# One pair of rotation tables, and a fixed engine for each step of the rotation, in an attention and two-MoE kernel

## The chip, the cores and the metric

The kernel runs on one NeuronCore of a Trainium2 chip. Its engines are TensorE (PE in the profile; PEld is its weight load), VectorE (DVE), ScalarE (ACT), GpSimd (POOL) and SyncE (SP), which here issues the DMA transfers. The metric is the device time of one execution in microseconds, lower is better.

## The reference

Attention over batch 4, 8 heads, 576 positions, head size 64, with rotary embedding of queries and keys; then a dense MoE layer with squared ReLU, then a second MoE layer with 8 experts of which each token takes one.

```python
def rotate(x):
    x1, x2 = (x[..., :half], x[..., half:])
    return np.concatenate([x1 * cos - x2 * sin, x1 * sin + x2 * cos], axis=-1)
q_rot, k_rot = (rotate(q), rotate(k))
scores = scale * np.matmul(q_rot, k_rot.transpose(0, 1, 3, 2))
scores = scores - np.max(scores, axis=-1, keepdims=True)
attn = np.exp(scores)
attn = attn / (np.sum(attn, axis=-1, keepdims=True) + 1e-09)
attn_out = np.matmul(attn, v)
...
h = x @ w_in;  r = np.maximum(h, 0.0);  x = (r * r) @ w_out     # 2304 x 512, d_ff 2048
...
for e in range(E):                                              # 8 experts, F 1024
    h = np.maximum(x[mask] @ w1[e], 0.0)
    out[mask] = gate_w[mask, None] * eom[mask, e, None] * (h @ w2[e])
```

## The kernel before

**Precision.** TensorE multiplies in fp32r. Each fp32 operand is split into a high part (a cast to fp32r) and a low part (the operand less its high part), and products are added up from two or three of the combinations. So nearly every tile in front of TensorE costs one cast and one subtraction.

**Attention.** The 32 heads are worked in 16 pairs p. `prepare(p)` loads the pair's keys and queries (`load(i)`: i = 1 for the keys, 0 for the queries), swaps neighbouring rows (`swap`, VectorE), multiplies x and the swapped x by a table each (`mul`, L295), adds them (`add`, L299) and splits the result. The table tile `tabs` has four parts of 128 x 576: cosine and sine times −1/√64 for the queries, cosine and sine for the keys. Each is a transfer of its own, in the first pair only. For the keys the high and low part go into the tile `hl` (`high_k`, `low_k`), and `fan(j)` copies them by DMA (L324, four transfers for a pair) into the operand tile `d`, to both halves of the partitions. For the queries `high_q` and `low_q` write `d` directly, one half of the partitions (one head) at a time. `ends_` copies the last 64 query rows of both heads into the tile `dz`. The values are split into `vh` (`v_high`, `v_low`).

`unit(P, p, c)` then does for each of five query chunks: `scores` (PE, L401, L409), the row minimum (`least`, DVE, L416; scores carry the minus sign), the exponential (`exponential`, ACT, L422), transposes of the probabilities (`turned`, L456; `remainder`, L461), their high part `phi` (cast, L209) and low part `plo` (DVE, L212), and the product with the values (L557 to L562). Line 209 is the helper for all casts and copies of ACT and DVE, L207 the one for POOL, L212 the one for all subtractions; in the profile they are told apart by the tiles.

**Which engine.** The strings `ROPE`, `SPLIT`, `TURN` and `SHIFT` name for every pair and step an engine (v VectorE, a ScalarE, p GpSimd). Before, they are long and differ from pair to pair; the first pair has strings of its own.

**The order.** Nothing is ordered by hand. `plan.add(engine, cost, emit, key, deps, slots)` notes each step; `Plan.emit` goes through a model of the engines in which each one takes, of the steps that are ready, the one with the lowest key, and writes the instructions in the order of the planned starts. On the chip every engine, and SyncE's queue of transfers, runs its instructions in that order, each waiting for its data. `KEYS` holds the keys by kind of step, `TAIL` and `LATE` those of the last block's rows and of the late units. Costs are in ns.

**The MoE stages.** Weights of the first MoE come as raw 64-bit words and are converted by ACT and DVE (`add_conversion`: L662 to L693, and L212 into `pg`), two half steps for each of 16 slices f. Two slices have pages from the start, two more once all pairs are prepared (`gate0`), twelve once the attention is over (`gate1`). `add_block(0)` starts when the first tokens' sums are loaded back and split (POOL, L754, L757, L212 into `xlo`); L787 and L817 are its products. Blocks 1 to 4, the routing and the expert units follow.

Of the kernel before, what the change touches and what calls it, by code (L numbers as in the profile page):

```python
# [40 lines left out]
BIG_MAX = (NT - EARLY * (BLK[3][0] // E) + E * 127) // UNIT  # L41
NH = 2 * (EARLY + LATE_MAX)
KF = F2 // 128
ROPE, SPLIT, TURN, SHIFT = "ppvpvvvpppvppppvvppppvpppppvppppppppppppppvpppppvpppppppppppppppppppppppvppppppppppppppppppppppp", "pppvvvaappvppappapppppppavppapvvppppavpppppappapppppapaappapppppapppppappappppaappppappppppappvp", "vvaavaaaavaaavaaaaaaavaaaaaaaaavavaaavaaaaaaaaaaavaaaaaaavaavaaaaaaavvvaaaaaaaavvvaaaaavaaaaaaavaaaaaaaaavvaavaaaaaaaaaaaaavaaaavaaaaaaaaavaaaaaaaavaaaaavaaaaaaaaavavaaaaaaaaaaavaaaaaaaavaaaaa", "aaaaaaaaaaaaaaaaaaaavaaaaavaavvaaaaaaaaaaaavaavaaaaaaavaaaaaaaav"
F64_TINY = 1.125 * 2.0**-15


TAIL, LATE = -10142, -11286
HI, LO = "aaavaaav", "vpvvvpvv"
DMA_RATE = 241  # L50
AHEAD = dict(DVE=10, ACT=14)
BEGIN = (4, 6, 6, 1)
SECOND = "ap"
KEYS = dict(fan=-84975, swap=32320, step=73908, conv=54493, x0=22475, end=-86588, load=-5688, rope=106951, qk=-63351, v=-40073, s=-11980, min=4893, exp=18765, rc=-77484, t=9315, hi=9602, lo=-12270, pv=18619, x=-74523)


def f32(ap):
    return ap.bitcast(F32)
# [18 lines left out]
def act(n):  # L77
    return 93 + n / 1.2
# [119 lines left out]
def two_moe_kernel(ctx, tc, qk, v, tab, cst, w_in, w_out, wg, w1, w2, out):  # L198
# [51 lines left out]
    def add_attention(ctx, rest, first):  # L250
# [21 lines left out]
        def prepare(p):  # L272
# [8 lines left out]
            def load(i):  # L281

                if "x" not in T:
                    T["x"] = pre.tile([128, 4, S], F32, tag="x", name="x", bufs=2)
                sp.dma_start(out=T["x"][:, 2 * i], in_=qk[p, :, i])
                if first:
                    for z in (2 * i, 2 * i + 1):
                        sp.dma_start(out=tabs[:, z], in_=tab[:, z])

            def swap(i):  # L290
                ve.stream_shuffle(out=T["x"][:, 2 * i + 1], in_=T["x"][:, 2 * i], mask=[j ^ 1 for j in range(32)])  # L291
# [1 line left out]
            def mul(i):  # L293
                x = T["x"]
                eng(3 * (i // 2) + i % 2).tensor_tensor(out=x[:, i], in0=x[:, i], in1=tabs[:, i], op=ALU.mult)  # L295
# [5 lines left out]
            def operand():  # L301
                if "d" not in T:
                    T["d"] = two.tile([128, 2, 3, S], F32R, tag="d", name="d")
                return T["d"]
# [12 lines left out]
            def low_q(j, on):  # L317
                h, o = slice(64 * j, 64 * j + 64), slice(64 - 64 * j, 128 - 64 * j)
                sub(ve if on == "v" else po, T["d"][o, j, 0], T["x"][h, 0], f32(T["d"][h, j, 0]))

            def fan(j):
                h = slice(64 * j, 64 * j + 64)
                for u in (0, 64):
                    sp.dma_start(out=f32(operand()[u:u + 64, j, 1:3]), in_=f32(T["hl"][h]))  # L324

            on, split = ("vvvvvv", "aavvap") if first else (choice(ROPE, p, 6), choice(SPLIT, p, 6))
            eng = lambda i: ve if on[i] == "v" else po
# [2 lines left out]
            parts = {}  # L330
            for i in (1, 0):
                k = key + KEYS["rope"] - i
                o = plan.add("SP", 3670 if first else 1220, lambda i=i: load(i), key + KEYS["load"] - i, fanned, [xs])
                m = [plan.add("DVE", dve(S), lambda i=i: swap(i), key + KEYS["swap"] - i, [o], [xs])]
                m.append(plan.add(*price(3 * i), lambda z=2 * i: mul(z), k, [o, m[0]], [xs]))
                m[0] = plan.add(*price(3 * i + 1), lambda z=2 * i + 1: mul(z), k, m[:1], [xs])
                o = plan.add(*price(3 * i + 2), lambda i=i: add(i), k, m, [xs])
                k = key + KEYS["qk"] - i
                if i:
                    a = plan.add(*copy_price(split[1], S), high_k, k, [o], [xs, hls])  # L340
                    b = plan.add(*sub_price(split[3], S), low_k, k, [a], [xs, hls])
                    T["fan"] = [plan.add("SP", 2444, lambda j=j: fan(j), key + KEYS["fan"], [a, b], [hls, ds]) for j in range(2)]
                    if first:
                        fanned.append(~T["fan"][1])
                else:
                    T["q"] = []
                    for j in range(2):
                        e = split[0] + split[2] if j == 0 else SECOND[2 * (p % (len(SECOND) // 2)):][:2]
                        if first:
                            e = "av" if j else "av"  # L350
                        a = plan.add(*copy_price(e[0], S), lambda j=j, e=e: high_q(j, e[0]), k, [o], [xs, ds])
                        b = plan.add(*sub_price(e[1], S), lambda j=j, e=e: low_q(j, e[1]), k, [a], [xs, ds])
                        T["q"].append([a, b])
# [16 lines left out]
            zs = ring_z.take()  # L370

            def ends_():
                copy(
                    on_ends, out=ends_q.rearrange("p j (a q) -> p (j a) q", a=2)[:, 0:4:3], in_=f32(T["d"][:, :, 0, 512:S])
                )

            on_ends = "a" if p == 0 else "p"
            T["end"] = plan.add(*copy_price(on_ends, 128), ends_, key + KEYS["end"], T["q"][0] + T["q"][1] + zeros, [ds, zs])
            T["slots"] = ds, vs, ring_sm.take(), zs
            prepared.extend([*T["fan"], *T["q"][0], *T["q"][1], T["vl"]])  # L380
            begin.append(T["fan"])
            return T

        def unit(P, p, c):
# [7 lines left out]
            for j in range(1 if both else 2):  # L392
                ss = ring_s.take()

                def scores(j=j):
                    d = P["d"]
                    t = T["s", j] = ps_s.tile([128, 2, 512], F32, tag="s", name="sc")
                    for hf in range(2):
                        z = slice(hf * HB, hf * HB + HB)
                        for part in (1, 2):  # L400
                            te.matmul(  # L401
                                out=t[:, hf, 0:HB], lhsT=ends_q[:, 1] if both else d[:, j, 0, q0:q0 + n],
                                rhs=d[:, 1 if both else j, part, z], start=part == 1, stop=part == 2 and not both,
                            )
                        if both:

                            for o, k0, m in ((0, 512, 64), (64, 0, HB - 64)) if hf == 0 else ((0, HB - 64, HB),):
                                for part in (1, 2):
                                    te.matmul(  # L409
                                        out=t[:, hf, o:o + m], lhsT=ends_q[:, 0], rhs=d[:, 0, part, k0:k0 + m],  # L410
                                        start=False, stop=part == 2 and o + m == HB,
                                    )

                def least(j=j):
                    T["mx", j] = small.tile([128, 1], F32, tag="mx", name="mx")
                    ve.tensor_reduce(out=T["mx", j], in_=T["s", j][:, :, 0:HB], axis=AX.XY, op=ALU.min)  # L416

                def exponential(j=j):
                    if j == 0:
                        T["pt"] = two.tile([128, 2, S], F32, tag="p", name="pt", bufs=3)  # L420
                    i = 5 * j + c
                    se.activation(  # L422
                        out=T["pt"][:, j].rearrange("p (a b) -> p a b", a=2), in_=T["s", j][:, :, 0:HB],
                        func=AF.Exp, bias=T["mx", j], scale=-1.0, accum_out=sums[p % 2][:, i:i + 1],
                    )

                ds, _, sms, zs = P["slots"]
                if both:
                    a = plan.add("PE", 1270, scores, key + KEYS["s"], [P["end"], *P["fan"]], [ss, ds, zs])
                else:  # L430
                    a = plan.add("PE", 4 * pe(HB), scores, key + KEYS["s"], [P["fan"][j], *P["q"][j]], [ss, ds])
                b = plan.add("DVE", 667, least, key + KEYS["min"], [a], [ss])
                ends.append(plan.add("ACT", 730, exponential, key + KEYS["exp"], [b] + ends, [ss, ps_, sms]))
                scored.append(ends[-1])
                P.setdefault("ends", []).append(ends[-1])
# [1054 lines left out]
def _shape_constants():  # L1490
# [3 lines left out]
    cos, sin = np.cos(freqs).T, np.sin(freqs).T  # L1494
    c = np.tile(np.stack([cos, cos], axis=1).reshape(D, S), (2, 1))
    s = np.tile(np.stack([-sin, sin], axis=1).reshape(D, S), (2, 1))
    g = np.float32(-1.0 / np.sqrt(D))
    tab = np.stack([c * g, s * g, c, s], axis=1).astype(np.float32)
    tab[64:, 2:] = np.roll(tab[64:, 2:], 64, axis=2)
    cst = np.zeros((128, 128 + 256 + E + 128 + NH + NRT), np.float32)  # L1500
    cst[:, 0:128] = np.eye(128)
    cst[:, 128:256] = np.triu(np.ones((128, 128)), 1)
# [12 lines left out]
def _layout(q, k, v, moe_w_in, moe_w_out, moe2_w_gate, moe2_w_output_gate, moe2_w1, moe2_w2):  # L1515

    qk = np.stack([q, k]).reshape(2, NP, 2, S, 2, D // 2).transpose(1, 2, 5, 4, 0, 3).reshape(NP, 128, 2, S)
    qk[:, 64:, 1] = np.roll(qk[:, 64:, 1], 64, axis=2)
    vp = v.reshape(NP, 2, S, D)
    vl = np.zeros((NP, 128, 11, D), v.dtype)  # L1520
    for j in range(2):
# [29 lines left out]
```

## Time and profile before

| | |
|---|---|
| median of 3 runs | 1007.44 us (1007.02 to 1008.35) |
| the profiled execution | 1005.06 us |
| its span, first to last instruction | 1003.2 us |
| busy: TensorE, VectorE, ScalarE, GpSimd | 933.9, 717.0, 529.7, 355.3 us |
| TensorE's mean granted clock | 0.992 of full speed |
| DMA | 117.70 MB, mean 117 GB/s |

Busy time is the time in which an engine executes; the rest of the span it waits or has nothing to do. Instructions of one engine may overlap a little at their ends, so that the sum of their durations is above its busy time. "x <- y" in a row means that the instruction writes x and reads y, or, in brackets behind an idle time, that y released the engine.

### The profile page before, as it was taken

The numbers are of one execution on the slowest core, as the hardware profiler recorded it, in microseconds if no ns is written. First come the engines' busy times: TensorE is split into PE (matmuls) and PEld (weight loads), VectorE is DVE, ScalarE is ACT, GpSimd is POOL, SyncE is SP. The second block draws the span as 40 slices with busy tenths as digits, with TensorE's granted clock in tenths as the row PEclk, the third lists the DMA queues.
The fourth block names the chain that finished last, engine by engine and source line by source line (L and its number), as shares of the span: only waits on it lengthen the run. The fifth ranks groups of instructions, "written<-read, shape, count | busy, mean of one in ns | idle before, by whom it ended". The sixth has DMA issues, their size and how long they took to land.

```text
span 1003.2 us, 16374 instructions
## 1 busy us (share of the span) xinstructions
PE 933.9 (93%) x5612; PEld 818.5 (82%) x5612; DVE 717.0 (71%) x1346; ACT 529.7 (53%) x1109; POOL 355.3 (35%) x277
## 2 busy tenths in 40 slices
PE   0799889998999999999999999999999999999995
PEld 0689888898888888778877887788998898999985
DVE  4989999999999999753255225444586999366666
ACT  1688878897888778521232123212463455244443
POOL 1789966998956000000000000000031455134342
PEclk9999999999999999999999999999999999999998
DMA  6466755765656665130022003000560613452611
GB/s 178 115 164 191 182 162 145 188 165 153 179 138 185 215 222 176 51 118 1 0 86 72 1 1 90 6 0 22 181 219 23 219 54 100 144 166 89 206 53 34
DMA packets 56616, 117.70 MB, mean 117 GB/s; under 512 B 9137, under 2 KB 18881, under 8 KB 56513
## 3 DMA queue, kind: packets, MB, share of 16 engines
q1 hardware_dynamic: 53232, 105.94, 36.1%
q0 software_dynamic: 3280, 10.49, 3.2%
q8 instruction: 52, 0.85, 0.4%
q14 instruction: 52, 0.42, 0.1%
HBM read 99.55 MB, written 19.21 MB: 118 GB/s over the span
## 4 chain that ended last, share of the span: by engine, by line
PE 71%; DVE 10%; ACT 5%; DMA 5%; issue 3%; POOL 3%; SPq 2%; DVEq 0%; POOLq 0%; ACTq 0%
PE h L787 20%; PE a L817 19%; PE h L1305 10%; PE a L1342 10%; PE sc L401 4%; DVE plo L212 2%; PE tp L456 2%; ACT pt L422 2%; DVE mx L416 2%; PE ov L557 2%; ACT phi L209 1%; POOL x L295 1%; DVE pg L212 1%; PE m L894 1%; DMA d<-hl 1%
## 5 line engine op out<-in xcount | busy, mean ns | idle before, releaser
L787 PE MATMUL h<-xhi,pg 128*128 128x512 f32 (+1 forms) x640 | 198.8, 374 | 0.0
L817 PE MATMUL a<-gh,pg 128*128 128x512 f32 (+1 forms) x640 | 196.2, 373 | 0.0
L1259 POOL DMA_INDIRECT raw<-x1d,gidx x22 | 22.7, 1033 | 373.8 <-DVE ssc L243 356.8
L794 ACT ACTIVATE r<-h 128x512 f32<-128x512 f32 (+1 forms) x80 | 44.3, 554 | 192.0 <-PE h L787 178.6
L401 PE MATMUL sc<-d 128*128 128x288 f32 x512 | 100.8, 321 | 41.2 <-DVE d L212 24.4
L787 PEld LDWEIGHTS h<-xhi,pg 128*128 128x128 f32 x640 | 117.3, 188 | 23.1
L817 PEld LDWEIGHTS a<-gh,pg 128*128 128x128 f32 x640 | 117.2, 188 | 22.1
L802 DVE TENSOR_TENSOR r<-r 128x512 f32<-128x512 f32 (+1 forms) x64 | 40.1, 626 | 124.1 <-ACT gh L798 124.1
L817 PE MATMUL a<-gl,pg 128*128 128x512 f32 (+1 forms) x320 | 119.6, 374 | 1.9 <-DVE gl L212 1.7
L422 ACT ACTIVATE pt<-sc,mx 128x576 f32<-128x576 f32 x144 | 107.5, 748 | 23.8 <-DVE mx L416 22.8
L1305 PE MATMUL h<-raw,pg 128*128 128x256 f32 x960 | 117.8, 283 | 2.1 <-ACT y L1349 1.3
L1305 PEld LDWEIGHTS h<-raw,pg 128*128 128x128 f32 x960 | 116.6, 191 | 3.4 <-issue 1.7
L787 PE MATMUL h<-xlo,pg 128*128 128x512 f32 (+1 forms) x320 | 118.9, 372 | 0.0
L401 PEld LDWEIGHTS sc<-d 128*128 128x128 f32 x512 | 75.5, 195 | 50.5 <-DVE d L212 24.8
L416 DVE TENSOR_REDUCE mx<-sc 128x1 f32<-128x576 f32 x144 | 105.8, 748 | 5.0 <-PE sc L401 4.5
L212 DVE TENSOR_TENSOR plo<-tp,phi 128x512 fp32r<-128x512 f32 x144 | 95.9, 678 | 4.4 <-ACT phi L209 3.7
L212 DVE TENSOR_TENSOR pg<-pg,pg 128x512 fp32r<-128x512 f32 x102 | 92.7, 933 | 4.1 <-ACT pg L209 3.7
L456 PE MATMUL tp<-ident,pt 128*128 128x128 f32 x576 | 87.5, 279 | 3.4 <-DVE plo L212 3.0
L295 POOL TENSOR_TENSOR x<-x,tabs 128x576 f32<-128x576 f32 x51 | 77.8, 1538 | 9.5 <-DVE x L291 4.7
L209 ACT CAST phi<-tp 128x512 fp32r<-128x512 f32 x125 | 72.2, 588 | 14.4 <-PE tp L456 13.8
L212 POOL TENSOR_TENSOR pg<-pg,pg 128x512 fp32r<-128x512 f32 x34 | 47.6, 1403 | 87.4 <-ACT pg L209 87.3
L456 PEld LDWEIGHTS tp<-ident,pt 128*128 128x128 f32 x576 | 70.1, 143 | 6.0 <-issue 2.4
(224 smaller groups left out, 1761.7 us busy)
## 6 DMA issues: line engine op xcount, KB each, us to landing
pg<-w_dram SPq DMA_DIRECT2D x176, 256.0 KB
d<-hl SPq DMA_DIRECT2D x64, 288.0 KB
x<-qk_dram SPq DMA_DIRECT2D x32, 288.0 KB
xtd<-xt SPq DMA_DIRECT2D x32, 288.0 KB
raw<-w_in_dram SPq DMA_DIRECT2D x16, 512.0 KB
raw<-w_out_dram SPq DMA_DIRECT2D x16, 512.0 KB
vr<-v_dram SPq DMA_DIRECT2D x16, 352.0 KB
x1d<-b SPq DMA_DIRECT2D x18, 256.0 KB
```

Source lines behind the costliest of these rows:

```text
L209: (ve.tensor_copy if on == "v" else se.copy)(out=out, in_=in_)
L212: eng.tensor_tensor(out=out, in0=a, in1=b, op=ALU.subtract)
L295: eng(3 * (i // 2) + i % 2).tensor_tensor(out=x[:, i], in0=x[:, i], in1=tabs[:, i], op=ALU.mult)
L401: te.matmul(out=t[:, hf, 0:HB], lhsT=ends_q[:, 1] if both else d[:, j, 0, q0:q0 + n], rhs=d[:, 1 if both else j, part, z], start=part == 1 ...
L416: ve.tensor_reduce(out=T["mx", j], in_=T["s", j][:, :, 0:HB], axis=AX.XY, op=ALU.min)
L422: se.activation(out=T["pt"][:, j].rearrange("p (a b) -> p a b", a=2), in_=T["s", j][:, :, 0:HB], func=AF.Exp, bias=T["mx", j], scale=-1.0, ...
L456: te.transpose(out=t[:, k], in_=T["pt"][:, j, i:i + 128], identity=ident)
L787: te.matmul(out=G["t"], lhsT=a[:, 128 * c:128 * c + 128], rhs=m[:, c, :n], start=c == 0 and i == 0, stop=c == KC - 1 and i == 2,)
L794: se.activation(out=G["r"], in_=G["t"], func=AF.Relu)
L817: te.matmul(out=T["acc", d][:, :n], lhsT=a[:, 128 * d:128 * d + 128], rhs=m, start=f == 0 and i == 0, stop=f == NF - 1 and i == 2,)
L1305: te.matmul(out=T["t"][:, f], lhsT=m[:, z], rhs=r[:, c], start=i == 0, stop=i == 11)
L1342: te.matmul(out=T["t"], lhsT=a[:, k, 128 * i:128 * i + 128], rhs=m, start=k == 0 and y == 0, stop=k == KF - 1 and y == 2,)
```

## The change

The tables come as one pair, cosine and sine, in one transfer; the queries' pair is made of it on ScalarE (`scale_tables`). To use one pair for both, the queries of the second head are now laid out with the same roll by 64 positions as its keys. In the first pair the keys' parts are no longer copied by DMA: `first_high` (ScalarE) and `first_low` (VectorE) write them to both halves of the partitions, and the load of the queries hangs in the plan on the keys' sum. From the second pair on GpSimd does all products and sums of the rotation, all subtractions for keys, queries and values and the high part of the values, and ScalarE all other high parts, all casts of the probabilities and all copies of the output. `ends_` is two copies instead of one. All keys have new values.

```diff
-ROPE, SPLIT, TURN, SHIFT = "ppvpvvvpppvppppvvppppvpppppv...", "pppvvvaappvppappap...", "vvaavaaaavaaavaa...", "aaaaaaaaaaaaaaaaaaaavaaaaavaavv..."
+ROPE, SPLIT, TURN, SHIFT = "pppppp", "aapppp", "aaaaaaaaaaaa", "aaaa"
-TAIL, LATE = -10142, -11286
+TAIL, LATE = -332229, -479512
-KEYS = dict(fan=-84975, swap=32320, step=73908, conv=54493, x0=22475, end=-86588, load=-5688, rope=106951, qk=-63351, v=-40073, s=-11980, min=4893, exp=18765, rc=-77484, t=9315, hi=9602, lo=-12270, pv=18619, x=-74523)
+KEYS = dict(fan=-213982, swap=238988, step=201344, conv=238593, x0=399905, end=-631240, load=-373541, rope=-65135, qk=-119699, v=-65126, s=-122507, min=-216773, exp=-122385, rc=-253869, t=350365, hi=-152247, lo=-190621, pv=489233, x=-165917)
...
                 sp.dma_start(out=T["x"][:, 2 * i], in_=qk[p, :, i])
-                if first:
-                    for z in (2 * i, 2 * i + 1):
-                        sp.dma_start(out=tabs[:, z], in_=tab[:, z])
+                if first and i:
+                    sp.dma_start(out=tabs[:, 2:4], in_=tab)
...
+            def first_high(j, u):
+                h, o = slice(64 * j, 64 * j + 64), slice(64 * u, 64 * u + 64)
+                se.copy(out=operand()[o, j, 1], in_=T["x"][h, 2])
+
+            def first_low(j, u):
+                h, o = slice(64 * j, 64 * j + 64), slice(64 * u, 64 * u + 64)
+                sub(ve, operand()[o, j, 2], T["x"][h, 2], f32(T["d"][h, j, 1]))
...
+            def scale_tables():
+                se.activation(out=tabs[:, 0:2], in_=tabs[:, 2:4], func=AF.Copy, scale=-(D ** -0.5))
...
-                o = plan.add("SP", 3670 if first else 1220, lambda i=i: load(i), key + KEYS["load"] - i, fanned, [xs])
+                o = plan.add("SP", 3670 if first and i else 1220, lambda i=i: load(i), key + KEYS["load"] - i, fanned, [xs])
+                if first and i:
+                    tables = plan.add("ACT", act(2 * S), scale_tables, key + KEYS["qk"], [o], [])
+                ready = [tables] if first and not i else []
...
-                if i:
+                if i and first:
+                    T["fan"] = []
+                    for j in range(2):
+                        made_ = []
+                        for u in range(2):
+                            a = plan.add("ACT", act(S), lambda j=j, u=u: first_high(j, u), k, [o], [xs, ds])
+                            made_ += [a, plan.add("DVE", dves(S), lambda j=j, u=u: first_low(j, u), k, [a], [xs, ds])]
+                        T["fan"].append(made_)
+                    fanned.append(o)
+                elif i:
...
-                    if first:
-                        fanned.append(~T["fan"][1])
...
-    g = np.float32(-1.0 / np.sqrt(D))
-    tab = np.stack([c * g, s * g, c, s], axis=1).astype(np.float32)
-    tab[64:, 2:] = np.roll(tab[64:, 2:], 64, axis=2)
+    tab = np.stack([c, s], axis=1).astype(np.float32)
+    tab[64:] = np.roll(tab[64:], 64, axis=2)
...
-    qk[:, 64:, 1] = np.roll(qk[:, 64:, 1], 64, axis=2)
+    qk[:, 64:] = np.roll(qk[:, 64:], 64, axis=3)
```

## Rows read from the trace of the kernel before

**Rows 1.** The page: busy us (share of the span) and instructions of TensorE first.

```profile
PE 933.9 (93%) x5612; PEld 818.5 (82%) x5612; DVE 717.0 (71%) x1346; ACT 529.7 (53%) x1109; POOL 355.3 (35%) x277
```

**Rows 2.** Stages from:to: length, busy us of each engine, clock, DMA share, GB/s.

```profile
40.00:320.00 280.00, 258.05 (x1923) 242.14 (x1922) 267.45 (x452) 236.03 (x566) 229.26 (x175) 0.99 0.64 170
326.00:417.00 91.00, 90.91 (x398) 73.83 (x397) 88.54 (x159) 68.85 (x121) 0.00 (x0) 1.00 0.53 169
```

**Rows 3.** Chain that ended last, first 30 us: start, length, what.

```profile
1.64 3.62 DMA tabs<-tab_dram
...
5.28 0.77 DVE x L295
...
6.07 0.77 DVE x L299
...
8.35 0.54 SPq L324
...
11.93 1.33 SPq L285
...
29.12 0.62 DVE mx L416
```

**Rows 4.** The opening in order of time: start, length, engine, line, operation.

```profile
0.72 0.40 SPq L285 DMA_DIRECT2D x<-qk_dram  x1
...
3.58 0.79 DVE L291 STREAM_SHUFFLE x<-x 128x576 f32<-128x576 f32 x1
...
7.57 0.76 DVE L212 TENSOR_TENSOR hl<-x,hl 128x576 fp32r<-128x576 f32 x1 [0.74 <-ACT hl L209]
...
19.78 0.76 DVE L295 TENSOR_TENSOR x<-x,tabs 128x576 f32<-128x576 f32 x1 [0.96 <-DMA tabs<-tab_dram]
...
21.36 1.36 ACT L209 CAST d<-x 64x576 fp32r<-64x576 f32 x2
...
22.98 2.71 DVE L212 TENSOR_TENSOR d<-x,d 64x576 fp32r<-64x576 f32 x2
...
23.87 1.33 PE L401 MATMUL sc<-d 128*128 128x288 f32 x4 [23.87 <-DVE d L212]
```

**Rows 5.** GpSimd's groups, 0 to 330 us: busy us, mean ns, idle before.

```profile
L295 POOL TENSOR_TENSOR x<-x,tabs 128x576 f32<-128x576 f32 x51 | 77.8, 1538 | 9.5 <-DVE x L291 4.7 <-issue 3.7 <-POOL d L212 0.7
L299 POOL TENSOR_TENSOR x<-x 128x576 f32<-128x576 f32 x30 | 45.9, 1532 | 19.4 <-DVE x L295 18.9
L212 POOL TENSOR_TENSOR d<-x,d 64x576 fp32r<-64x576 f32 x30 | 42.9, 1428 | 3.1 <-ACT d L209 0.8
...
L207 POOL TENSOR_SCALAR dz<-d 128x128 fp32r<-128x128 f32 x15 | 6.0, 400 | 3.1 <-PE sc L409 3.0
L207 POOL TENSOR_SCALAR d<-x 64x576 fp32r<-64x576 f32 x8 | 5.8, 730 | 0.3
...
L207 POOL TENSOR_SCALAR vh<-vr 128x704 fp32r<-128x704 f32 x6 | 5.1, 845 | 0.1
L207 POOL TENSOR_SCALAR hl<-x 128x576 fp32r<-128x576 f32 x5 | 3.4, 673 | 0.0
```

**Rows 6.** Order of time: GpSimd's last query subtractions; TensorE's first MoE product.

```profile
287.10 2.92 POOL L212 TENSOR_TENSOR d<-x,d 64x576 fp32r<-64x576 f32 x2
...
326.00 0.39 PE L787 MATMUL h<-xhi,pg 128*128 128x512 f32 x1
```

**Rows 7.** VectorE's groups, 0 to 330 us.

```profile
L209 DVE CAST phi<-tp 128x512 fp32r<-128x512 f32 x19 | 13.0, 682 | 0.1
L295 DVE TENSOR_TENSOR x<-x,tabs 128x576 f32<-128x576 f32 x13 | 11.1, 861 | 1.6 <-DMA tabs<-tab_dram 1.4
L666 DVE SCALAR_TENSOR_TENSOR m<-m,raw 128x512 f32<-128x512 f32 x10 | 10.8, 1078 | 0.0
```

**Rows 8.** VectorE, the same conversion step in the first MoE block, 326 to 417 us.

```profile
L666 DVE SCALAR_TENSOR_TENSOR m<-m,raw 128x512 f32<-128x512 f32 x24 | 16.2, 684 | 0.7 <-ACT m L662 0.6
```

**Rows 9.** ScalarE, casts of 64 rows, 0 to 330 us.

```profile
L209 ACT CAST d<-x 64x576 fp32r<-64x576 f32 x23 | 15.4, 670 | 0.9 <-issue 0.4
```

More of the change, by code (lines that the diff above doesn't have):

```diff
@@ L43 @@
 KF = F2 // 128
-ROPE, SPLIT, TURN, SHIFT = "ppvpvvvpppvppppvvppppvpppppvppppppppppppppvpppppvpppppppppppppppppppppppvppppppppppppppppppppppp", "pppvvvaappvppappapppppppavppapvvppppavpppppappapppppapaappapppppapppppappappppaappppappppppappvp", "vvaavaaaavaaavaaaaaaavaaaaaaaaavavaaavaaaaaaaaaaavaaaaaaavaavaaaaaaavvvaaaaaaaavvvaaaaavaaaaaaavaaaaaaaaavvaavaaaaaaaaaaaaavaaaavaaaaaaaaavaaaaaaaavaaaaavaaaaaaaaavavaaaaaaaaaaavaaaaaaaavaaaaa", "aaaaaaaaaaaaaaaaaaaavaaaaavaavvaaaaaaaaaaaavaavaaaaaaavaaaaaaaav"
+ROPE, SPLIT, TURN, SHIFT = "pppppp", "aapppp", "aaaaaaaaaaaa", "aaaa"
 F64_TINY = 1.125 * 2.0**-15
-TAIL, LATE = -10142, -11286
+TAIL, LATE = -332229, -479512
 HI, LO = "aaavaaav", "vpvvvpvv"
@@ L332, in prepare @@
                 k = key + KEYS["rope"] - i
-                o = plan.add("SP", 3670 if first else 1220, lambda i=i: load(i), key + KEYS["load"] - i, fanned, [xs])
+                o = plan.add("SP", 3670 if first and i else 1220, lambda i=i: load(i), key + KEYS["load"] - i, fanned, [xs])
+                if first and i:
+                    tables = plan.add("ACT", act(2 * S), scale_tables, key + KEYS["qk"], [o], [])
+                ready = [tables] if first and not i else []
                 m = [plan.add("DVE", dve(S), lambda i=i: swap(i), key + KEYS["swap"] - i, [o], [xs])]
-                m.append(plan.add(*price(3 * i), lambda z=2 * i: mul(z), k, [o, m[0]], [xs]))
-                m[0] = plan.add(*price(3 * i + 1), lambda z=2 * i + 1: mul(z), k, m[:1], [xs])
+                m.append(plan.add(*price(3 * i), lambda z=2 * i: mul(z), k, [o, m[0], *ready], [xs]))
+                m[0] = plan.add(*price(3 * i + 1), lambda z=2 * i + 1: mul(z), k, [m[0], *ready], [xs])
                 o = plan.add(*price(3 * i + 2), lambda i=i: add(i), k, m, [xs])
                 k = key + KEYS["qk"] - i
-                if i:
+                if i and first:
[8 more added lines that the diff above has]
+                elif i:
                     a = plan.add(*copy_price(split[1], S), high_k, k, [o], [xs, hls])
                     b = plan.add(*sub_price(split[3], S), low_k, k, [a], [xs, hls])
-                    T["fan"] = [plan.add("SP", 2444, lambda j=j: fan(j), key + KEYS["fan"], [a, b], [hls, ds]) for j in range(2)]
-                    if first:
-                        fanned.append(~T["fan"][1])
+                    T["fan"] = [[plan.add("SP", 2444, lambda j=j: fan(j), key + KEYS["fan"], [a, b], [hls, ds])] for j in range(2)]
                 else:
@@ L372, in ends_ @@
             def ends_():
-                copy(
-                    on_ends, out=ends_q.rearrange("p j (a q) -> p (j a) q", a=2)[:, 0:4:3], in_=f32(T["d"][:, :, 0, 512:S])
-                )
+                for j in range(2):
+                    copy(on_ends, ends_q[:, j, 64 * j:64 * j + 64], f32(T["d"][:, j, 0, 512 - 512 * j:S - 512 * j]))
             on_ends = "a" if p == 0 else "p"
-            T["end"] = plan.add(*copy_price(on_ends, 128), ends_, key + KEYS["end"], T["q"][0] + T["q"][1] + zeros, [ds, zs])
+            T["end"] = plan.add(copy_price(on_ends, 64)[0], 2 * copy_price(on_ends, 64)[1], ends_, key + KEYS["end"], T["q"][0] + T["q"][1] + zeros, [ds, zs])
             T["slots"] = ds, vs, ring_sm.take(), zs
-            prepared.extend([*T["fan"], *T["q"][0], *T["q"][1], T["vl"]])
-            begin.append(T["fan"])
+            prepared.extend([*T["fan"][0], *T["fan"][1], *T["q"][0], *T["q"][1], T["vl"]])
+            begin.append(T["fan"][0] + T["fan"][1])
             return T
@@ L401, in scores @@
                             te.matmul(
-                                out=t[:, hf, 0:HB], lhsT=ends_q[:, 1] if both else d[:, j, 0, q0:q0 + n],
+                                out=t[:, hf, 0:HB], lhsT=ends_q[:, 1] if both else d[:, j, 0, q0 + 64 * j:q0 + 64 * j + n],
                                 rhs=d[:, 1 if both else j, part, z], start=part == 1, stop=part == 2 and not both,
@@ L428, in unit @@
                 if both:
-                    a = plan.add("PE", 1270, scores, key + KEYS["s"], [P["end"], *P["fan"]], [ss, ds, zs])
+                    a = plan.add("PE", 1270, scores, key + KEYS["s"], [P["end"], *P["fan"][0], *P["fan"][1]], [ss, ds, zs])
                 else:
-                    a = plan.add("PE", 4 * pe(HB), scores, key + KEYS["s"], [P["fan"][j], *P["q"][j]], [ss, ds])
+                    a = plan.add("PE", 4 * pe(HB), scores, key + KEYS["s"], [*P["fan"][j], *P["q"][j]], [ss, ds])
                 b = plan.add("DVE", 667, least, key + KEYS["min"], [a], [ss])
```

## The prediction

> **What bounds the kernel now.** I read the page first: TensorE is busy 93% of the span [rows 1], so a gain can only come out of the 69 us in which it is idle. The table by stage says where these lie. Up to 24 us TensorE has nothing to do; its first score product starts at 23.87 us [rows 4]. From 40 to 320 us, the attention of the 16 head pairs, it is busy 258.05 of 280 us, so 22.0 us are idle, and VectorE is the fuller engine with 267.45 us (ScalarE 236.03, GpSimd 229.26) [rows 2]. From 326.0 us on, when the first MoE block's products begin [rows 6], TensorE runs nearly without a gap: 90.91 of 91.0 us in the first block, where VectorE has 88.54 us of weight conversion and splitting beside it [rows 2]. So I treat the 677.2 us from 326.0 to the end (1003.2) as a piece that is moved as a whole, and ask by how much its start moves.
>
> The opening is read from the chain of waits and the order in time [rows 3, 4]. Keys: load, two tables (landing at 5.26), products, sum (6.07 to 6.84), high and low part, and at 8.35 SyncE begins four transfers that copy the split keys to where TensorE wants them. Their issue holds SyncE's queue until 11.93; only then does the load of the queries go out, followed by two more tables, the last of which VectorE awaits until 19.78. Then come sum, two ScalarE casts (21.36) and two VectorE subtractions (22.98), and the product at 23.87. After that VectorE first finishes other work, so the first minimum is at 29.12, over 5 us after the first score.
>
> **The change, part by part.**
>
> *Opening, keys.* Load and tables are the same bytes up to 5.26, but the two tables are now one transfer, so the first product can't start at 4.4, before the second table is there. Two products and a sum at 0.77 [rows 3] from 5.28: sum done at 7.6, 0.75 later than now. Then four ScalarE copies of 64 rows, at 0.67 each (the 23 casts of that shape) [rows 9]: to 10.3. The four subtractions on VectorE run behind them. Those of the second half need the fourth copy, so two remain after 10.3, at 0.76 (the one of 128 rows alone) [rows 4]: to 11.9. The bound from above is 1.34 each, half of the pair's 2.71 [rows 4], which ran while GpSimd worked.
>
> *Opening, queries.* With the four copies gone from SyncE's queue nothing in front of the query load waits, so it goes out behind the tables and is there long before 11.9. Were it held to the keys' sum, it would land at 7.6 plus 2.9 (0.72 to 3.58, the first load [rows 4]) = 10.5, still in time. The scaling of the tables on ScalarE (1152 elements; between one and two of the 0.67 casts) starts at about 5.3 and ends by 6.7, before the copies. So queries: shuffle 0.79, three steps at 0.77, from 11.9 to 15.0. Cast 0.67; a shuffle for the next pair may slip in front of the subtraction (0.79); the subtraction at 1.34, since GpSimd now rotates the second pair: 17.1. Bounds: 15.8 (nothing in front, 0.76) and 19 (all subtractions at 1.34). Gain 23.9 − 17.1 = 6.8, from 4.9 to 8.1.
>
> *First minimum.* The new keys rank the minimum ahead of the constants' conversion, which stands in front of it now. I expect it 2.2 us after the first score (a subtraction and a shuffle), not 5.2. Half of the 3 us comes back, since those conversions must still be done: gain 1.5, from 0 to 3.
>
> *VectorE, pairs 1 to 15.* Gone are nine of 13 products at 0.861 (four stay with the first pair) and 19 casts at 0.682 [rows 7]: 20.7 us, besides smaller casts and copies. VectorE drops from 267 to below 247 of 280 us and is no longer the fullest.
>
> *ScalarE.* It takes the 19 casts and nine of 64 rows (23 become 32), at about 0.67 [rows 9]: +18.8. Its 236 us become about 255 of 280, 91%: not the bound, but close enough that I don't count all of TensorE's idle time as won.
>
> *GpSimd.* It takes nine products and sums (81 become 90 at 1.535): +13.8; nine value copies at 0.845: +7.6; it gives eight query copies (5.8) and five key copies (3.4) to ScalarE; the small copy of the last query rows becomes two, +0 to +6.0, I take 3 [rows 5]. Together +15.2. In return it no longer waits for VectorE's products, 18.9 us in front of its sums [rows 5]. With a start some 7 us earlier its last query subtraction, which now ends at 290.0 [rows 6], would end at 290.0 − 7 + 15.2 − 18.9 = 279.3.
>
> Here a rule speaks against the change. The Trainium skill, GPSIMD Engine Reference, section 4.1 (Engine selection), assigns elementwise work to VectorE and calls GpSimd about twice as slow with two inputs. The trace agrees (1.535 against VectorE's 0.77 in the opening); by that rule alone the nine moved products cost more than they free, which would matter only if GpSimd sets the pace, and that is the second rival below.
>
> *Steady state.* Beyond the opening GpSimd's schedule gives 290.0 − 279.3 − 6.8 = 3.9 us; TensorE's idle time gives at most 22.0. The lead of GpSimd (36 us, 290.0 to 326.0 [rows 6]) may shrink somewhat, so I take 8, nearer to GpSimd's end. The lower bound isn't zero: the second rival gives time back.
>
> *Moved without a price.* The other keys (load, conversions, block 0's input, the last block's rows, the late units) keep their rank among what is ready on the same engine, as far as I can order them: GpSimd's rotations are all done before block 0's input is asked for. Sixty instead of 64 copies and one table transfer instead of four take DMA time only in the opening. If the order of the later stages does shift, I allow 3 us either way.
>
> *Sum.* 6.8 + 1.5 + 8 = 16.3: span 1003.2 to 986.9, the profiled execution 1005.06 to 988.8. The median of the runs shown stands 2.4 above that execution: 991.1, rounded to 991.
>
> **The rivals.**
>
> *Only the opening pays.* TensorE's idle time between 40 and 320 stays, because its cause is the relay score, minimum, exponential, and not a full VectorE. For it: VectorE's weight conversions are filler that could have waited. Against it: GpSimd's 18.9 us. Time: 1007.4 − 8.3 = 999.
>
> *GpSimd sets the pace (slower).* Every one of its 45 subtractions for pairs 1 to 15 now waits for a ScalarE cast, and the new keys rank those casts behind exponentials and probability casts, where they stood ahead; ScalarE's queue in turn is blocked when a cast stands in it before GpSimd's sum is ready. If GpSimd needs its present lead, the gain of 10.7 in its schedule is used up by 0.24 us per cast. A wait of 0.67 (one other ScalarE instruction) each is 30 us: block 0 starts 19 later, 1026; half of it is 15, 4 us later, 1012. Against it: now GpSimd waits for a cast for under 1 us in all in front of its 30 query subtractions [rows 5].
>
> *Weights come late.* VectorE's conversion steps take 1.078 during attention and 0.684 in the first block, when GpSimd is idle [rows 7, 8]. More GpSimd work stretches them, and in block 0 VectorE has no room (88.54 of 91.0). What would slip is at most eight half steps of five instructions, 27 us at 0.68; half of it, 13, gives 1004. Against it: VectorE is freed of over 20 us. The Trainium skill, SBUF — State Buffer, section "SBUF: two separate sides", describes the cause as an exclusive lock: a GpSimd instruction and a VectorE one with two SBUF inputs wait for each other whole. By that rule VectorE would lose up to a whole GpSimd instruction each time; the 1.078 against 0.684 agrees with some such waits.
>
> **How the numbers follow.** Chances: forecast 0.62, with its own range of 980 to 1000; only the opening 0.14 (999); GpSimd sets the pace 0.16 (1012, to 1026); late weights 0.08 (1004). A measurement of this kernel can tell about 0.2% (2 us) from no change; the three runs shown spread over 1.3 us. Faster: 0.62 + 0.12 of the second + 0.04 of the fourth = 0.78. Within 0.2%: 0.02 + 0.02 + 0.03 = 0.07. Slower: 0.14 + 0.01 = 0.15. The range 979 to 1010 reaches past no change into the slower cases and leaves out some 0.17.
>
> **What would show it.** Right: the first score near 17 us and the first minimum about 2 us behind; no wait of GpSimd's sums for VectorE; VectorE clearly under TensorE from 40 to 300; the first MoE product near 310; from there to the end 677 us as now. Wrong: GpSimd near 99% in every slice with TensorE waiting for its subtractions; exponentials behind casts that wait for GpSimd; TensorE gaps in the first block behind converted weights; or a last stretch that is longer.

## The result, and the profile after

The changed kernel takes 982.75 us (982.1 to 984.54, median of 4 runs), the kernel before 1007.25 beside it: ratio 0.9758, 95% interval 0.9741 to 0.9774. That is 24.5 us less where 16 were forecast, inside the range. The profiled execution takes 982.75 us, with a span of 980.9.

The page after, busy time by engine (compare [rows 1]):

```profile
span 980.9 us, 16444 instructions
...
PE 929.2 (95%) x5612; PEld 815.6 (83%) x5612; DVE 702.0 (72%) x1304; ACT 545.4 (56%) x1154; POOL 364.6 (37%) x297
```

The opening after, in order of time (compare [rows 4]):

```profile
2.12 0.43 SPq L285 DMA_DIRECT2D x<-qk_dram  x1
...
5.22 1.16 ACT L335 ACTIVATE tabs<-tabs 128x1152 f32<-128x1152 f32 x1 [3.21 <-DMA tabs<-tab_dram]
...
7.55 2.73 ACT L322 CAST d<-x 64x576 fp32r<-64x576 f32 x4 [1.17 <-DVE x L298]
...
11.87 0.81 DVE L290 STREAM_SHUFFLE x<-x 128x576 f32<-128x576 f32 x1
...
16.24 5.18 POOL L294 TENSOR_TENSOR x<-x,tabs 128x576 f32<-128x576 f32 x3 [2.87 <-DVE x L290]
16.91 3.23 DVE L212 TENSOR_TENSOR d<-x,d 64x576 fp32r<-64x576 f32 x2
...
18.31 1.33 PE L422 MATMUL sc<-d 128*128 128x288 f32 x4 [18.31 <-DVE d L212]
20.06 0.74 DVE L437 TENSOR_REDUCE mx<-sc 128x1 f32<-128x576 f32 x1
...
24.36 1.35 DVE L437 TENSOR_REDUCE mx<-sc 128x1 f32<-128x576 f32 x2
```

The query load goes out at 2.12 instead of 11.93, since nothing that waits stands in front of it in SyncE's queue; that the plan hangs it on the keys' sum set only its place in the order, since that sum ends later, at 7.5. The keys are written by the engines from 7.55 on, the queries follow at 11.87, and the first score starts at 18.31 instead of 23.87: 5.6 us earlier. The first minimum follows after 1.75 us, but the next ones only at 24.36, because the conversion of the constants has moved in between: the second exponential starts at 25.09 instead of 30.50, 5.4 us earlier, no more than the first score.

The two parts of the span, from the first score to the first product of the first MoE block and from there to the end, before and then after (columns: from:to, length, then busy us of TensorE, its weight load, VectorE, ScalarE, GpSimd; granted clock; DMA):

```profile
23.90:326.00 302.10, 273.10 (x2005) 255.50 (x2005) 287.67 (x484) 246.90 (x592) 246.84 (x187) 0.99 0.62 164
326.00:1003.20 677.20, 660.77 (x3610) 562.97 (x3608) 419.79 (x846) 278.80 (x512) 105.86 (x85) 0.99 0.29 94
```

```profile
18.30:305.70 287.40, 269.52 (x2016) 254.18 (x2017) 272.17 (x444) 259.01 (x633) 255.41 (x206) 1.00 0.65 172
305.70:980.90 675.20, 659.66 (x3599) 561.44 (x3597) 417.27 (x841) 279.13 (x512) 104.77 (x86) 0.99 0.29 95
```

Of the 22.3 us that the span is shorter, 5.6 come from the first score, 14.7 from the attention behind it (302.1 to 287.4), and 2.0 from all the rest. In the attention TensorE's idle time falls from 29.0 to 17.9 us, and its busy time by 3.6. VectorE is not emptier in proportion: 272 of 287 us are still 95%.

What has gone from TensorE's idle time are above all waits for exponentials, which fell by 10.2 of the 11.1 us (waits of scores for the exponential that frees their place, before and then after: us in all, times, longest):

```profile
PE sc L401 <- ACT pt L422: 16.5, 23, 3.6
```

```profile
PE sc L422 <- ACT pt L443: 6.3, 10, 2.1
```

GpSimd's groups in the first 330 us after (compare [rows 5]):

```profile
L294 POOL TENSOR_TENSOR x<-x,tabs 128x576 f32<-128x576 f32 x60 | 87.6, 1475 | 5.0 <-DVE x L290 4.7
L298 POOL TENSOR_TENSOR x<-x 128x576 f32<-128x576 f32 x30 | 44.6, 1488 | 0.9
L212 POOL TENSOR_TENSOR d<-x,d 64x576 fp32r<-64x576 f32 x30 | 43.5, 1451 | 13.3 <-ACT d L209 10.0 <-DVE plo L212 0.9 <-PE tp L477 0.7
...
L207 POOL TENSOR_SCALAR dz<-d 128x64 fp32r<-128x64 f32 x30 | 7.6, 271 | 0.0
```

The 18.9 us in front of the sums, in which GpSimd waited for VectorE's products, are gone; 10.0 us for ScalarE's casts have come.

### The profile page after: what moved, and what is told of

It is laid out like the page before. It is cut to its first block, busy times and chain, and to the rows that moved or that the text cites. A ratio compares the mean times of both kernels' runs of the same rounds, so it can differ in the third digit from the quotient of the medians.

```text
span 980.9 us, 16444 instructions
## 1 busy us (share of the span) xinstructions
PE 929.2 (95%) x5612; PEld 815.6 (83%) x5612; DVE 702.0 (72%) x1304; ACT 545.4 (56%) x1154; POOL 364.6 (37%) x297
## 4 chain that ended last, share of the span: by engine, by line
PE 76%; DVE 14%; ACT 4%; DMA 2%; issue 2%; POOL 1%; SPq 0%; DVEq 0%; ACTq 0%; POOLq 0%
PE h L808 20%; PE a L838 19%; PE h L1326 11%; PE a L1363 10%; PE sc L422 4%; PE ov L578 3%; DVE mx L437 3%; PE tp L477 3%; DVE plo L212 3%; ACT pt L443 2%; DVE pg L212 1%; ACT phi L209 1%; DVE x L290 1%; PE m L915 1%; PE m L1294 1%
## 5 line engine op out<-in xcount | busy, mean ns | idle before, releaser
L422 PE MATMUL sc<-d 128*128 128x288 f32 x512 | 99.9, 319 | 26.8 <-DVE d L212 18.9
L443 ACT ACTIVATE pt<-sc,mx 128x576 f32<-128x576 f32 x144 | 107.9, 750 | 12.4 <-DVE mx L437 11.8
L294 POOL TENSOR_TENSOR x<-x,tabs 128x576 f32<-128x576 f32 x60 | 87.6, 1475 | 5.0 <-DVE x L290 4.7
L209 ACT CAST phi<-tp 128x512 fp32r<-128x512 f32 x144 | 83.1, 588 | 6.2 <-PE tp L477 5.6
```

The lines of the kernel that those rows point to most:

```text
L209: (ve.tensor_copy if on == "v" else se.copy)(out=out, in_=in_)
L422: te.matmul(out=t[:, hf, 0:HB], lhsT=ends_q[:, 1] if both else d[:, j, 0, q0 + 64 * j:q0 + 64 * j + n], rhs=d[:, 1 if both else j, part, z ...
L443: se.activation(out=T["pt"][:, j].rearrange("p (a b) -> p a b", a=2), in_=T["s", j][:, :, 0:HB], func=AF.Exp, bias=T["mx", j], scale=-1.0, ...
```

## The experiments

Reading this result as my prediction does (theory A: the parts add up, keys cost nothing) calls for taking the change apart. It has three parts that can be put in or left out alone: the opening (one table pair, engine-written keys, the queries' roll, `ends_` as two copies), the engine strings, and the keys (with `TAIL` and `LATE`). Six kernels complete the eight combinations. Each is one of the two kernels with the other's lines, as here for the opening alone:

```diff
 # the changed kernel, with
-ROPE, SPLIT, TURN, SHIFT = "pppppp", "aapppp", "aaaaaaaaaaaa", "aaaa"
+ROPE, SPLIT, TURN, SHIFT = "ppvpvvvppp...", "pppvvvaapp...", "vvaavaaaav...", "aaaaaaaaaa..."
-KEYS = dict(fan=-213982, swap=238988, ...)      # TAIL, LATE too
+KEYS = dict(fan=-84975, swap=32320, ...)
```

**opening_alone.** 

> The changed kernel's opening (one table pair, keys of the first pair written by the engines, queries' roll) with the engine strings and the keys of the kernel before. Theory A (the parts add up: opening some 8 to 9 us, fixed engines the rest, keys nothing): 997 to 1000 us, first score near 18 us. Theory B (the fixed engines pay only with the keys that fit them): the same 997 to 1000 here. Rival C (GpSimd's schedule governs until the first MoE block, so an earlier first score is lost again): 1004 or more.

**engines_alone** (the strings' two lines the other way, on the kernel before). 

> Only the four engine strings of the changed kernel; opening and keys as before. A: 992 to 1000 us, GpSimd's waits for VectorE's products gone. B: 1005 or slower, since casts, rotations and values are then ranked for another distribution.

**keys_alone** (the lines of `KEYS`, `TAIL` and `LATE`, on the kernel before). 

> Only the keys (with TAIL and LATE) of the changed kernel; opening and engine strings as before. A and B: 1004 to 1012 us, no gain. Rival D (the order of the minima, casts and loads is what pays): 990 to 998.

**opening_engines** (the changed kernel with the old lines of `KEYS`, `TAIL`, `LATE`). 

> The changed kernel with the keys of the kernel before. A: 982 to 986 us, as the changed kernel's 982.75. B and D: 992 or more, the opening's gain alone.

These four came back at 1030.25, 1012.34, 1020.97 and 1004.46 us, and with them fell theory A: none of the parts pays alone, and the two that I had priced (opening and engines) give 0.4% together. B has the sign of that, but not that an opening or keys alone cost 21 and 13 us (by the ratios in the table below); C's bound holds, but it expected a gain to be lost and not a loss; D falls with the keys alone. Theory E was formed here: an order that was searched for one whole kernel fits that kernel only.

**no_opening** (the kernel before with the new strings, `KEYS`, `TAIL` and `LATE`). 

> The changed kernel's engine strings and keys with the opening of the kernel before (four tables, the first pair's keys copied by DMA). A' (the opening is worth what it moves the first score, about 6 us, and up to 9 with the first minimum): 988 to 992 us. E (an order searched for one whole kernel fits that kernel alone, so that undoing any part costs more than the part): 996 or more, with the stage from the first score to the first MoE product longer than the changed kernel's 287.4 us.

**no_engines** (the changed kernel with the old strings). 

> The changed kernel's opening and keys with the engine strings of the kernel before. A' (fixed engines free VectorE of 20 us, of which some 8 to 13 reach the end): 991 to 996 us. E: 1005 or more, as with the opening alone.

All eight together. "Stage" is the time from the first score to the first MoE product, "rest" from there to the end of the span, both of the profiled execution:

| opening | engines | keys | us | ratio to before (95%) | first score | stage | rest |
|---|---|---|---|---|---|---|---|
| old | old | old | 1007.25 | 1 | 23.9 | 302.1 | 677.2 |
| new | old | old | 1030.25 | 1.0208 (1.0169 to 1.0248) | 18.2 | 334.8 | 676.5 |
| old | new | old | 1012.34 | 1.0049 (1.0032 to 1.0065) | 24.5 | 311.2 | 676.0 |
| old | old | new | 1020.97 | 1.0125 (1.0086 to 1.0164) | 24.6 | 320.8 | 675.0 |
| new | new | old | 1004.46 | 0.9964 (0.9948 to 0.9980) | 18.3 | 308.5 | 677.0 |
| old | new | new | 998.94 | 0.9898 (0.9865 to 0.9931) | 24.5 | 293.9 | 677.3 |
| new | old | new | 1020.83 | 1.0116 (1.0081 to 1.0150) | 18.3 | 325.2 | 674.9 |
| new | new | new | 982.75 | 0.9758 (0.9741 to 0.9774) | 18.3 | 287.4 | 675.2 |

no_opening and no_engines went to theory E: 998.94 and 1020.83 us, with stages longer than 287.4; A' falls with them.

In the table two columns hardly move. The rest lies between 674.9 and 677.3 in these eight, so it does move as a whole, as the prediction took it. The first score depends almost only on the opening, and is some 6 us earlier in every kernel with the new one. Everything else happens in the stage, and there the parts don't add up. With the old strings, a new opening or new keys lengthen it by 19 to 33 us; with the new strings and keys, the new opening shortens it by another 6.5 beside the 6 of the first score. Read by the strings, the table says more (by the ratios): the new ones cost 5 us with everything else old, but bring 25 us with the new opening, 23 with the new keys and 36 with both. And where the opening or the keys alone cost 21 and 13 us on the old strings, they bring 9 and 15 on the new ones.

With the old strings GpSimd, which has the other half of the same rotations, waits long for VectorE. First the opening alone, then the new opening and keys with the old strings:

```profile
POOL x L294 <- DVE x L290: 21.6, 7, 11.5
POOL x L298 <- DVE x L294: 12.2, 3, 9.0
```

```profile
POOL x L294 <- DVE x L290: 27.0, 4, 12.7
POOL x L298 <- DVE x L294: 15.2, 3, 12.2
```

GpSimd stands still for 34 and 42 us until VectorE has swapped rows or multiplied its share, in single waits of 9 to 12.7 us; in the changed kernel the two are 4.7 us and under 1. But that these waits lengthen the stage isn't shown, and three figures speak against it. In the kernel before they are 23.6 us (4.7 and 18.9, [rows 5]), and with the keys alone, where the stage is 19 us longer, hardly more, 25.7. GpSimd's lead, from its last query subtraction to the first MoE product, is 38 and 41 us in the two runs, not shorter than the 36 before. And TensorE waited with its scores for GpSimd's subtractions for 2.5 us only with the opening alone, for exponentials 26.0 us (16.5 before). Why a new opening or new keys cost so much with the old strings stays open.

With the new strings and the old keys GpSimd waits for something else, the value products of a pair two back, whose place in `vh` its value copies need. The run opening_engines, then engines_alone:

```profile
POOL vh L207 <- PE ov L581: 25.4, 8, 11.8
```

```profile
POOL vh L207 <- PE ov L560: 27.8, 7, 11.3
```

Here the old keys rank the value copies ahead of the rotation, the new ones just behind. Theory F takes this one rank as the cause.

**rope_before_values:**

```diff
 # opening_engines, with
-KEYS = dict(... rope=106951, ...)
+KEYS = dict(... rope=-40082, ...)     # v=-40073
```

> Opening and engines of the changed kernel, keys of the kernel before but for one: the rotation's key goes from behind the values' to just ahead of it, as the new keys have it, so GpSimd does a pair's rotation before its value copy. F (this one rank is what GpSimd lost in the run without the new keys, where its value copies waited 25.4 us for value products): 985 to 996 us, that wait nearly gone. E (the other ranks matter as much): 1000 or more.

Measured: 1008.06 us, ratio 0.9996 (0.9972 to 1.0020), stage 315.9. The wait for value products went down to 4.5 us (with one more of 9.6 us whose releaser the trace doesn't name), as F says, and the time did not follow. F falls, and E's bound of 1000 holds: taking most of that wait away gained nothing. TensorE's idle time in the stage is 38.7 us as against 37.7; it is spread over many short waits for exponentials and for GpSimd's query subtractions.

**min_after_low**, for theory D, one rank of the changed kernel put back:

```diff
 # the changed kernel, with
-KEYS = dict(... min=-216773, ...)
+KEYS = dict(... min=-180000, ...)     # lo=-190621
```

> The changed kernel with one key moved: the minimum ranks behind the probabilities' low parts (still ahead of the constants), as before. D (minima first keep the relay of score, minimum and exponential short): 988 to 996 us, exponentials waiting longer for minima than the changed kernel's 11.8 us. A' (ranks don't matter): 981 to 985.

Measured: 1000.72 us, ratio 0.9919 (0.9886 to 0.9951), stage 304.6: 16 us lost, by the ratios, through one rank, more than either theory had. But what D names as the reason isn't there. ScalarE's longest waits, this run first, then the changed kernel:

```profile
ACT phi L209 <- PE tp L477: 13.2, 26, 1.8
ACT pt L443 <- DVE mx L437: 10.2, 15, 3.4
```

```profile
ACT pt L443 <- DVE mx L437: 11.8, 15, 3.4
ACT phi L209 <- PE tp L477: 5.6, 17, 0.9
```

The exponentials wait no longer for the minima than before the move (10.2 against 11.8 us). TensorE's idle time in the stage rises from 17.9 to 31.0 us, spread over many short waits. So either the rank pays in another way, or any other order is worse. The last four kernels leave every rank, engine and instruction as it is and change only a price in the plan by 1 ns, so that the same keys give a somewhat different order.

**The nudges**, on the changed kernel and on the kernel before:

```diff
 # the two runs _pool, in pool2:
-    return 130 + 2.18 * n
+    return 131 + 2.18 * n
 # the two runs _act, in act:
-    return 93 + n / 1.2
+    return 94 + n / 1.2
```

after_nudge_pool: 

> The changed kernel, but the plan prices each two-input GpSimd step 1 ns higher, so it writes another order from the same keys; no work, engine or rank is changed. G (both kernels stand on an order picked by search, some 15 us better than a neighbour of the same make): 993 to 1005 us. A'' (fixed engines and keys' ranks make the time, the exact order doesn't matter): 981 to 986.

after_nudge_act: 

> The changed kernel with 1 ns more on each priced ScalarE step in the plan. G: 993 to 1005 us. A'': 981 to 986. With the minimum's rank (D) as the cause of the 18 us lost by ranking it behind the low parts, both nudges stay at 981 to 986.

before_nudge_pool: 

> The kernel before with the same 1 ns on GpSimd steps in the plan. G: 1013 to 1028 us, as the mixed kernels with its engine strings (1020 to 1030). A'': 1006 to 1009.

before_nudge_act: 

> The kernel before with the same 1 ns on ScalarE steps in the plan. G: 1013 to 1028 us. A'': 1006 to 1009.

| | us | ratio to before (95%) | stage | rest |
|---|---|---|---|---|
| after_nudge_pool | 988.64 | 0.9802 (0.9757 to 0.9846) | 292.5 | 676.4 |
| after_nudge_act | 996.39 | 0.9889 (0.9844 to 0.9934) | 294.2 | 681.8 |
| before_nudge_pool | 1008.16 | 1.0004 (0.9983 to 1.0026) | 303.1 | 677.5 |
| before_nudge_act | 1006.84 | 0.9992 (0.9972 to 1.0012) | 302.0 | 678.7 |

Theory G, that both kernels stand on a picked order, is wrong for the kernel before, and for the changed kernel it is borne out by one nudge of two: the second lies in its range, the first between both ranges. By the ratios the changed kernel loses 4 and 13 us to 1 ns in a price (0.9758 to 0.9802, with intervals that overlap, so that the 4 are not clear of noise, and to 0.9889); the kernel before loses nothing. In the changed kernel's profiled executions 5.1 and 6.8 us lie in the stage; the second nudge loses another 6.6 in the rest. So E's reason, that any change leaves a fitted order, doesn't explain why the opening or the keys alone cost the kernel before 21 and 13 us.

## Why the prediction was right, and where it was not

**First score: 17.1 forecast, 18.31 measured.** Right in its path: the keys are done and the queries begin at 11.87 (11.9 forecast), no entry of SyncE's queue stands any more in the chain between the tables and the first score, and all kernels with the new opening show the time. The edits of the opening weren't run one by one. The gain is 1.2 us smaller for two reasons, seen in the chain of the changed kernel: the two products took 1.95 us and not 1.54, and two shuffles for the next pair, not one, stand in front of the subtraction.

```profile
12.72 1.95 DVE x L294 x2
14.69 0.70 DVE x L298
15.38 1.49 DVE x L290 x2
16.91 1.34 DVE d L212
18.28 1.85 DVE d L212
```

The subtraction that the first score waits for took the 1.34 forecast; the longer one comes behind it. The bound of 15.8 was a slip: with the cast's 0.67 its own terms give 16.4.

**First minimum: 2.2 behind the score forecast, 1.75 measured.** Right. But of the 3 us all comes back at once, and not half: the second exponential is no earlier than the first score makes it.

**GpSimd: last query subtraction at 279.3 forecast, at 277.5 measured** (GpSimd in order of time, below). The end is near, but three errors cancel: the start moved by 5.6 us and not 7, the work grew by 8.6 and not 15.2 (90 rotation steps took 1.48 us and not 1.535, which is 5 of the 6.6), and the idle time up to that subtraction fell by 15.6 (37.5 to 21.9) and not 18.9.

```profile
276.07 1.40 POOL L212 TENSOR_TENSOR d<-x,d 64x576 fp32r<-64x576 f32 x1
```

**ScalarE at 91%: measured 259.0 of 287.4, 90%.** The share is right in part by luck: 12.1 us more and not 18.8, in a stage 14.7 us shorter.

**VectorE clearly under TensorE: wrong.** It is at 272.2 us in the stage, TensorE at 269.5. It lost 15.5 us, but its weight conversions took 47.6 us instead of 35.3, by the sum of their durations: 41 instructions instead of 37, at 1.16 us on the mean instead of 0.95. Nor does an emptier VectorE by itself shorten the stage: with the new opening and strings and the old keys it had 280.6 of 308.5 us, 91%, and the stage was 6 us longer than before.

**Steady state: 8 forecast; 1.5 and 8 stand against 14.7 measured.** This term is mis-sized, and its reason, an emptier VectorE and a GpSimd that no longer waits for it, isn't borne out as the cause. Opening and engines without the keys, which by my working hold all of the gain, give a stage of 308.5 us, 6 longer than before. The step that failed is "Moved without a price": new keys as such were put at nothing. The loads, which its sentence names as keeping their rank, don't keep it, and the ranks of casts and minima that the prediction did see entered the sum only with the first minimum. At least four ranks differ: on GpSimd rotations now stand ahead of values, on ScalarE key and query casts behind exponentials, on VectorE minima ahead of low parts, in SyncE's queue loads ahead of the key copies. With the new opening and strings, the new keys are worth 21 us (0.9964 to 0.9758), where the prediction's parts without them were to bring 16 and brought 4. So it is luck in good part that the sum came this near.

**The rest: 677 forecast, 675.2 measured**, within the 3 us allowed; the second nudge, with 681.8, shows that an order alone can move it further.

**The rivals.** Only the opening pays: refuted twice, since alone it costs 21 us and without it the kernel still gains 1.0%. GpSimd sets the pace: its sign, waits for casts, is there with 10.0 us in front of the query subtractions, against 0.8 before [rows 5], but its lead only fell from 36 to 28 us (277.5 to 305.7), and no wait of TensorE's scores for one of its steps is over 0.7 us. Late weights: the conversions are slower, as that rival says, but TensorE is busy 93.91 of the 94 us from 306 on.

```profile
306.00:400.00 94.00, 93.91 (x404) 75.64 (x403) 86.79 (x154) 71.02 (x124) 0.42 (x1) 1.00 0.56 173
```

**What stays open.** Of the 24.5 us, some 4 (not clear of noise) to 13 depend on the very order that these keys give, as the nudges show; 11 to 20 remain with a neighbouring order. In what way the new strings and keys together shorten TensorE's waits for exponentials is not shown. Whether a rank by itself, the minimum's above all, is worth anything beyond that can't be told: putting it back lost 16 us, the nudges up to 13. The other three ranks weren't undone one by one in the changed kernel. That a new search for the new strings with the old opening would find less than 998.94 wasn't tried either.

## What to carry to other kernels

When the order of instructions is planned from prices and keys, don't add up prices of the parts of a change: here each part alone cost 5 to 21 us and all three together gained 24. Run the parts in all combinations, and nudge a price by 1 ns to see how much hangs on the very order. Here a fixed engine for each step was the ground on which the other two parts paid; with steps shared piece by piece either of them, put in alone, cost time. An engine that is 95% full isn't the bound by that alone, and a long wait of an engine that is ahead (25 us of GpSimd's here) can go without any gain.

## What the runs showed of the hardware

Idle time of TensorE can cost twice. The stage holds the same matmuls in all these kernels, but TensorE is busy for 269.5 us of it in the changed kernel at a mean granted clock of 1.00, and for 286.2 with the opening alone at 0.95, a mean over the clock's two levels, 2.4 and 1.2 GHz. From 95 to 100 us of that kernel TensorE is idle for 2.65 us, in pieces; from 100 to 105 it isn't idle at all, but the clock is at 0.50, the lower level:

```profile
95.00:100.00 5.00, 2.35 (x14) 1.75 (x13) 4.38 (x5) 1.89 (x5) 5.00 (x4) 0.90 0.71 185
100.00:105.00 5.00, 5.00 (x24) 4.97 (x23) 1.75 (x3) 2.25 (x7) 3.87 (x5) 0.50 0.89 191
```

Of the 32.7 us by which its stage is longer than before, 13.1 are longer busy time and 19.6 idle time. The idle time of the whole stage doesn't settle what the clock does: with the keys alone it is 36.3 us, at a clock of 0.96 and 284.5 us busy; with the new opening and strings and the old keys it is 37.7 us, at 0.99 and 270.8 us busy.

A subtraction of 64 x 576 on VectorE took 0.76 us in the opening of the changed kernel before GpSimd's first one begins (two in a row, below), and up to 1.85 beside GpSimd's products (18.28 in the chain above, while GpSimd has products from 16.24 on).

```profile
8.26 1.52 DVE L212 TENSOR_TENSOR d<-x,d 64x576 fp32r<-64x576 f32 x2 [0.74 <-ACT d L322]
```
